# Where the intermediate word of a weight conversion lives: SBUF or PSUM

## The chip, the cores and the metric

One core of one Trainium2 chip runs the kernel. The metric is device time in microseconds (us), the median of three runs. The engines are called by the profile's names: PE (TensorE's matmuls), PEld (its weight loads), DVE (VectorE), ACT (ScalarE), POOL (GpSimd) and SP (SyncE, which issues most transfers).

## What is computed

Three layers follow each other. Attention has 4 sequences of 576 positions and 8 heads of 64, and each position sees the 64 positions up to its own. Its output, 2304 tokens of 512, goes through a dense layer, and that through a layer in which each token may choose one of eight experts:

```python
scores = scale * np.matmul(q, k.transpose(0, 1, 3, 2))
scores = np.where((rel >= 0) & (rel < 64), scores, -1000000000.0)
attn = np.exp(scores - max) / sum;  x = attn @ v          # (2304, 512)
h = x @ w_in                                              # 512 -> 2048, float64 weights
x = (np.maximum(h, 0.0) ** 2) @ w_out                     # 2048 -> 512
# experts: tokens with x @ w_skip > 0 take the expert of their largest gate logit
out = x.copy()
out[do_compute] = xc + gate_w * (np.maximum(xc @ w1[e], 0) @ w2[e])
```

The dense layer's weights come in as 64-bit numbers. Their two 32-bit words must be turned into a 32-bit float on the chip, before they can be multiplied.

## The kernel before

The 2304 tokens are 18 tiles of 128 and 9 chunks of two tiles. Attention of a tile is done in two groups of four heads' blocks. `at_qk` (L244) makes the scores in one PSUM bank, takes the row maximum on DVE (L268), the exponentials on ACT (L281), and normalizes on DVE (L285 to L288); `at_tr` (L292) transposes them into a bank that ACT reads out (L298); `at_pv` (L301) multiplies by v and splits the result into a high and a low part (ACT L322, DVE L323).

The dense layer runs in units (chunk, j) with eight j per chunk. `l1` (L447) takes 24 matmuls into a hidden bank (L443 to L445, tile `h`), ACT applies relu (L456) and square (L462), rounds to the high part (L463), and DVE makes the low part `gl` (L464). `l2` (L467) adds the products with the output weights to the accumulators `acc`. Units of chunks 0 and 1 alternate; l2 follows l1 by two units.

The conversion works on half a weight block at a time, 128 x 512 numbers: 32 halves in all, in the order i0, i1, o0, i2, o1, i3 and so on (i for input weights, o for output weights). `conv_load` (L184) orders a load of 512 KB on SP; five are under way at the start, and each conversion orders the next one when its last instruction is issued (L221, with a small GpSimd memset L193 behind it). `conv_next` (L199) turns a half into two float parts:

1. ACT L207 scales the high word, POOL L208 clamps it. Both work in place on `hw`.
2. DVE L210 shifts the high word left by 3 into `f`; DVE L212 merges the sign bit from `hw` into `f`; DVE L214 merges the top bits of the low word `lw` into `f`.
3. ACT L220 rounds `f` to the high part of the weight, POOL L221 subtracts to get the low part.

`f` is a tile of 128 x 512 words in SBUF, from a pool of NST = 3 buffers. Four conversions are called in the prologue (`PRO`: after steps 2, 4, 6 and 8 of ten, in which the eight groups of chunks 0 and 1 pass through `at_qk`, `at_tr` and `at_pv`). After that `inject` (L613) calls two in each unit: 4 in the first two units, and 24 in the next twelve.

PSUM has eight banks. Two belong to `ps_h` (hidden tiles, and the scores of chunks 0 and 1), two each to `ps_acc` and `ps_s` (accumulators of chunks 0 and 1, and their `at_pv`), and two to the pool `ps_a`. `psa()` (L91) hands out the tiles of `ps_a`, named `a`: the transpositions of all chunks and, from chunk 2 on, the scores and products of attention, and later the routing. The two banks of `ps_a2` are added only after the conversions. In `inject`, the attention of chunk 2 begins in the eleventh unit: its scores stand in units 10 to 13, ahead of those units' conversions, with the transposition of group n just ahead of the scores of group n + 1.

The last part of the kernel (L733 and L910) is in an order written by hand. All that comes before, the conversions among it, is put in order by a planner that goes by the order of the program as priority and by its own costs of instructions. On each engine the order is then fixed, and semaphores are the only waits.

Of the kernel before, what the change touches and what calls it, by code (L numbers as in the profile page):

```python
# [11 lines left out]
I32 = mybir.dt.int32  # L12
U32 = mybir.dt.uint32
AF = mybir.ActivationFunctionType
ALU = mybir.AluOpType
# [42 lines left out]
SIGN = -(1 << 31)  # L58
# [3 lines left out]
def body(ctx, tc, qt_d, kt_d, vw_d, wi_d, wo_d, w9_d, w9r_d, w1_d, w2_d, out):  # L62
# [28 lines left out]
    def psa():  # L91
        turn[0] += 1
        return ps_a[turn[0] // 2 % len(ps_a)].tile([P, 512], F32, tag="a", name="a")
# [90 lines left out]
    def conv_load(after=None):  # L184
        if not conv_q:
            return
        kind, j, half = conv_q.pop(0)
        tag = f"s{conv_n[0]}"
        conv_n[0] += 1
        raw = wp.tile([P, 512, 2], I32, tag=tag, name=f"r{kind}{j}_{half}")  # L190
        if after is not None:
            with tc.issue_after(after.ins):
                nc.gpsimd.memset(raw[:, 0, :], 0)  # L193
        nc.sync.dma_start(
            out=raw.rearrange("p a b -> p (a b)"),
            in_=(wi_d if kind == "i" else wo_d)[j, :, half * 1024:(half + 1) * 1024])
        raw_q.append((raw, tag, kind, j, half))

    def conv_next():  # L199
        if not raw_q:  # L200
            return
        raw, tag, kind, j, half = raw_q.pop(0)
        hw, lw = raw[:, :, 1], raw[:, :, 0]
        f = st.tile([P, 512], I32, tag="f", name="f")
        ff = f.bitcast(F32)
        hf = hw.bitcast(F32)
        nc.scalar.activation(out=hf, in_=hf, func=AF.Copy, scale=F64_SCALE)  # L207
        nc.gpsimd.tensor_scalar(  # L208
            out=hf, in0=hf, scalar1=F64_MAX, scalar2=-F64_MAX, op0=ALU.min, op1=ALU.max)
        nc.vector.tensor_scalar(  # L210
            out=f, in0=hw, scalar1=3, scalar2=None, op0=ALU.logical_shift_left)
        nc.vector.scalar_tensor_tensor(  # L212
            out=f, in0=hw, scalar=SIGN, in1=f, op0=ALU.bitwise_and, op1=ALU.bitwise_or)
        nc.vector.scalar_tensor_tensor(  # L214
            out=f, in0=lw, scalar=29, in1=f,
            op0=ALU.logical_shift_right, op1=ALU.bitwise_or)
        w_tag[kind, j, half] = tag
        w = wp.tile([P, 2, 512], F32R, tag=tag, name=f"w{kind}{j}_{half}")
        (wi_t if kind == "i" else wo_t)[j, half] = w
        nc.scalar.copy(out=w[:, 0, :], in_=ff)  # L220
        conv_load(nc.gpsimd.tensor_tensor(  # L221
            out=w[:, 1, :], in0=ff, in1=w[:, 0, :].bitcast(F32), op=ALU.subtract))
# [349 lines left out]
    if True:  # L572
# [27 lines left out]
        for s in range(10):  # L600
            if s < 8:
                qk[s]()
            if 1 <= s < 9:
                tr[s - 1]()
            if 2 <= s:
                pv[s - 2]()
            for _ in range(PRO[s]):
                conv_next()
# [4 lines left out]
        def inject(u, s):  # L613
            for op in slots.pop((u, s), ()):
                op()
            for _ in range(2 if u < 2 else 1):
                conv_next()
            v = u - first[NCH - 1]
            if v >= 0 and s == 1:
                for _ in range(EWV[v] if v < len(EWV) else 0):  # L620
                    ew_split()
                ew_pump(3 if v < NJ else NE + 1)

        n_u = len(units)
        for u in range(n_u):
            if u == first[2]:
# [5 lines left out]
                    out=w9b, in_=w9r_d.unsqueeze(0).to_broadcast([P, NE + 1, DM]))  # L632
# [100 lines left out]
        with tc.manual_schedule():  # L733
# [9 lines left out]
            for j in range(NJ - TAIL + 1, NJ - 1):  # L743
# [30 lines left out]
                out=id0, in0=pick, scalar1=float(FAR), scalar2=nearf, op0=ALU.add, op1=ALU.min)  # L774
# [4 lines left out]
                out=cnt, in0=pc[:, 0:NE], scalar1=float(P - 1), scalar2=None, op0=ALU.add)  # L779
            nc.vector.tensor_scalar(  # L780
                out=cnt, in0=cnt, scalar1=7, scalar2=None, op0=ALU.logical_shift_right)
# [187 lines left out]
```

## Time and profile before

| what | value |
|---|---|
| median of 3 runs | 689.13 us (687.75 to 691.53) |
| profiled execution | 687.76 us, its span 686.1 us |
| PE busy | 652.7 us, 95% of the span |
| DVE busy | 435.3 us, 63% |
| ACT busy | 355.1 us, 52% |
| POOL busy | 157.2 us, 23% |

The profile is one execution. Busy time is the time in which an engine works on an instruction; an instruction that stands still on a shared resource counts as busy. The shares are means over stages that have different limits, so the stretches and their waits are what is to be read.

### The profile page before, as it was taken

What the parts mean: (1) busy time and instruction counts of PE and PEld (TensorE: products, weight loads), DVE (VectorE), ACT (ScalarE), POOL (GpSimd) and SP (SyncE); (2) the same over time, 40 slices, a digit from 0 to 9 for tenths busy, and PEclk for the clock granted to TensorE, in tenths of its full rate; (3) what the DMA queues carried; (4) which work ended last, traced back from release to release, by engine and by line L of the source; (5) the groups of instructions that cost most, each with busy time, mean ns of one, the idle gap of its engine ahead of it and who ended that gap; (6) DMA issues with size and microseconds to landing.
All of it is one profiled execution on the core that took longest, in us unless ns stands there. A gap on an engine that the chain in (4) does not pass through costs nothing. (4 is left out here: it accounts for less than half of the span.)

```text
span 686.1 us, 12318 instructions
## 1 busy us (share of the span) xinstructions
PE 652.7 (95%) x4473; PEld 567.2 (83%) x4473; DVE 435.3 (63%) x1192; ACT 355.1 (52%) x819; POOL 157.2 (23%) x183
## 2 busy tenths in 40 slices
PE   6688999899999999999999999999999999999995
PEld 4577888789899999989899889989997777777774
DVE  5999999947726725824933942961644635278991
ACT  4776557544535535444444544453542535367861
POOL 5546566500100000000000010030011423024451
PEclk9899999999999999999999999999999999999999
DMA  8975344163213113122220310306584237738800
GB/s 293 266 234 192 124 154 141 45 230 102 55 46 101 48 54 89 44 70 68 64 70 31 101 41 30 114 19 208 192 280 166 63 125 277 297 116 294 305 15 8
DMA packets 51076, 88.70 MB, mean 129 GB/s; under 512 B 24046, under 2 KB 24302, under 8 KB 50864
## 3 DMA queue, kind: packets, MB, share of 16 engines
q1 hardware_dynamic: 47584, 83.38, 36.6%
q0 software_dynamic: 2976, 3.95, 1.8%
q8 instruction: 46, 0.75, 0.5%
q10 hardware_dynamic: 432, 0.32, 0.1%
q14 instruction: 38, 0.31, 0.1%
HBM read 79.07 MB, written 12.49 MB: 133 GB/s over the span
## 5 line engine op out<-in xcount | busy, mean ns | idle before, releaser
L443 PE MATMUL h<-xt,wi 128*128 128x256 f32 x576 | 164.1, 285 | 2.4 <-ACT r L456 2.4
L444 PE MATMUL h<-xt,wi 128*128 128x256 f32 x576 | 164.5, 286 | 0.0
L445 PE MATMUL h<-xt,wi 128*128 128x256 f32 x576 | 163.5, 284 | 0.0
L443 PE MATMUL acc<-wo,gh 128*128 128x512 f32 x288 | 115.9, 406 | 5.6 <-ACT wo L220 4.6
L443 PEld LDWEIGHTS h<-xt,wi 128*128 128x128 f32 x576 | 110.0, 191 | 6.0 <-ACT r L456 3.0
L444 PE MATMUL acc<-wo,gh 128*128 128x512 f32 x288 | 113.2, 394 | 0.1
L445 PE MATMUL acc<-wo,gl 128*128 128x512 f32 x288 | 112.6, 392 | 0.0
L444 PEld LDWEIGHTS h<-xt,wi 128*128 128x128 f32 x576 | 110.0, 191 | 2.5
L464 DVE TENSOR_TENSOR gl<-r,gh 128x512 fp32r<-128x512 f32 x72 | 53.8, 747 | 90.4 <-ACT gh L463 90.4
L445 PEld LDWEIGHTS h<-xt,wi 128*128 128x128 f32 x576 | 110.0, 191 | 0.5 <-POOL wi L221 0.2
L435 POOL DMA_INDIRECT tab_d<-route,posi x18 | 19.5, 1083 | 355.6 <-DVE posi L426 263.7
L456 ACT ACTIVATE r<-h 128x512 f32<-128x512 f32 x72 | 42.5, 594 | 97.8 <-PE h L445 94.1
L354 DVE CUSTOM_DVE_ANT_0 prod<-sm,w9b 128x512 f32<-128x512 f32 x108 | 73.9, 684 | 1.9 <-ACT sm L331 1.5
L443 PEld LDWEIGHTS acc<-wo,gh 128*128 128x128 f32 x288 | 53.9, 189 | 15.3 <-ACT wo L220 5.3
L445 PEld LDWEIGHTS acc<-wo,gl 128*128 128x128 f32 x288 | 54.1, 188 | 12.1 <-DVE gl L464 0.4
L444 PEld LDWEIGHTS acc<-wo,gh 128*128 128x128 f32 x288 | 54.4, 189 | 8.5 <-POOL wo L221 0.2
L521 DVE TENSOR_TENSOR e_s<-e_s,e_s 128x1024 fp32r<-128x1024 f32 x34 | 45.6, 1361 | 12.2 <-ACT e_s L519 11.8
L281 ACT ACTIVATE sm<-sm,nmx 128x128 f32<-128x128 f32 x96 | 37.5, 392 | 20.7 <-DVE nmx L275 20.3
L462 ACT ACTIVATE r<-r 128x512 f32<-128x512 f32 x72 | 45.3, 632 | 1.4
L298 ACT COPY sm<-a 128x512 f32<-128x512 f32 x36 | 21.2, 588 | 46.9 <-PE a L296 46.9
L463 ACT CAST gh<-r 128x512 fp32r<-128x512 f32 x72 | 44.5, 619 | 1.5
L519 ACT CAST e_s<-e_s 128x1024 fp32r<-128x1024 f32 x42 | 43.0, 1051 | 2.5 <-PE acc L445 2.0
(200 smaller groups left out, 1154.0 us busy)
## 6 DMA issues: line engine op xcount, KB each, us to landing
e_s<-in_w_dram SPq DMA_DIRECT2D x54, 512.0 KB, 5.5
v<-in_vw_dram SPq DMA_DIRECT2D x18, 512.0 KB, 3.6
ri<-in_wi_dram SPq DMA_DIRECT2D x16, 512.0 KB, 5.3
ro<-in_wo_dram SPq DMA_DIRECT2D x16, 512.0 KB, 3.5
k<-in_kt_dram SPq DMA_DIRECT2D x18, 384.0 KB, 3.9
e_r<-in_w_dram SPq DMA_DIRECT2D x10, 512.0 KB, 6.4
qpad<-in_qt_dram SPq DMA_DIRECT2D x36, 128.0 KB, 3.6
x_d<-sm SPq DMA_DIRECT2D x17, 256.0 KB, 2.1
```

Of the source, the lines that this page charges most:

```text
L281: nc.scalar.activation(out=e[:, u, :], in_=s[:, u * P:(u + 1) * P] if early else e[:, u, :], func=AF.Exp, bias=nmx[:, u:u + 1], scale=1.0 ...
L298: nc.scalar.copy(out=pt, in_=pp)
L354: nc.vector.tensor_tensor_reduce(out=prod, in0=x2_t[t], in1=w9b_t[0][:, j, :], scale=1.0, scalar=0.0, op0=ALU.mult, op1=ALU.add, accum_out ...
L443: nc.tensor.matmul(out_ap, lhsT=ah, rhs=bh, start=start, stop=False)
L444: nc.tensor.matmul(out_ap, lhsT=ah, rhs=bl, start=False, stop=False)
L445: nc.tensor.matmul(out_ap, lhsT=al, rhs=bh, start=False, stop=stop)
L456: nc.scalar.activation(out=r, in_=hp.rearrange("p a b -> p (a b)"), func=AF.Relu)
L462: nc.scalar.activation(out=r, in_=r, func=AF.Square)
L463: nc.scalar.copy(out=ghf, in_=r)
L464: nc.vector.tensor_tensor(out=glf, in0=r, in1=ghf.bitcast(F32), op=ALU.subtract)
L519: nc.scalar.copy(out=hi, in_=raw)
L521: eng.tensor_tensor(out=lo, in0=raw, in1=hi.bitcast(F32), op=ALU.subtract)
```

## The change

The intermediate word gets a tile `fp` from `psa()`, read as 32-bit integers. L210 writes `fp` instead of `f`; L212 reads and writes `fp`; L214 reads `fp` and writes `f` in SBUF as before. The other inputs (`hw`, `lw`) stay in SBUF, and ACT L220 and POOL L221 read `f` as before. 32 tiles more are drawn from the two banks of `ps_a`.

```diff
         hw, lw = raw[:, :, 1], raw[:, :, 0]
+        fp = psa().bitcast(I32)
         f = st.tile([P, 512], I32, tag="f", name="f")
...
         nc.vector.tensor_scalar(
-            out=f, in0=hw, scalar1=3, scalar2=None, op0=ALU.logical_shift_left)
+            out=fp, in0=hw, scalar1=3, scalar2=None, op0=ALU.logical_shift_left)
         nc.vector.scalar_tensor_tensor(
-            out=f, in0=hw, scalar=SIGN, in1=f, op0=ALU.bitwise_and, op1=ALU.bitwise_or)
+            out=fp, in0=hw, scalar=SIGN, in1=fp, op0=ALU.bitwise_and, op1=ALU.bitwise_or)
         nc.vector.scalar_tensor_tensor(
-            out=f, in0=lw, scalar=29, in1=f,
+            out=f, in0=lw, scalar=29, in1=fp,
             op0=ALU.logical_shift_right, op1=ALU.bitwise_or)
```

## Rows read from the trace of the kernel before

**Rows 1.** Stretches: from:to, length, busy PE, PEld, DVE, ACT, POOL (count), PEclk, DMA, GB/s.
```profile
10.00:36.00 26.00, 17.86 (x148) 14.98 (x149) 23.61 (x44) 20.07 (x81) 12.40 (x17) 0.80 1.00 312
36.00:142.00 106.00, 97.79 (x717) 86.50 (x714) 99.04 (x126) 68.63 (x159) 61.39 (x74) 1.00 0.44 143
...
200.00:500.00 300.00, 300.00 (x2231) 271.60 (x2230) 166.23 (x690) 144.65 (x374) 15.78 (x22) 1.00 0.25 79
```

**Rows 2.** Waits of PE, 36 to 142 us: total us, times, longest us.
```profile
PE acc L443 <- ACT wo L220: 4.6, 4, 1.4
PE h L443 <- ACT r L456: 2.4, 1, 2.4
PE a L296 <- DVE sm L288: 1.1, 2, 0.7
```

**Rows 3.** Waits of PE, 8 to 36 us.
```profile
PE a L296 <- DVE sm L288: 3.2, 4, 1.3
```

**Rows 4.** Waits of ACT, 8 to 142 us.
```profile
ACT wo L220 <- DVE f L214: 13.1, 9, 3.1
```

**Rows 5.** DVE groups by form, 0 to 142 us: count, busy us, mean ns, idle before.
```profile
L214 DVE SCALAR_TENSOR_TENSOR f<-ri,f 128x512 int32<-128x512 int32 x16 | 17.9, 1120 | 0.3
L214 DVE SCALAR_TENSOR_TENSOR f<-ro,f 128x512 int32<-128x512 int32 x16 | 17.1, 1070 | 0.4
L212 DVE SCALAR_TENSOR_TENSOR f<-ri,f 128x512 int32<-128x512 int32 x16 | 16.1, 1004 | 0.4
L212 DVE SCALAR_TENSOR_TENSOR f<-ro,f 128x512 int32<-128x512 int32 x16 | 14.6, 915 | 0.3
L464 DVE TENSOR_TENSOR gl<-r,gh 128x512 fp32r<-128x512 f32 x15 | 14.5, 967 | 3.7 <-ACT gh L463 3.7
...
L210 DVE TENSOR_SCALAR f<-ro 128x512 int32<-128x512 int32 x16 | 11.8, 739 | 0.6 <-POOL ro L208 0.6
L210 DVE TENSOR_SCALAR f<-ri 128x512 int32<-128x512 int32 x16 | 8.3, 517 | 0.3 <-POOL ri L208 0.3
```

**Rows 6.** DVE groups by form, 142 to 500 us.
```profile
L464 DVE TENSOR_TENSOR gl<-r,gh 128x512 fp32r<-128x512 f32 x54 | 37.2, 689 | 80.2 <-ACT gh L463 80.2
```

**Rows 7.** Timeline of DVE, 60 to 65 us: start, duration, instruction.
```profile
60.50 1.65 DVE L214 SCALAR_TENSOR_TENSOR f<-ri,f 128x512 int32<-128x512 int32 x1
62.07 0.41 DVE L210 TENSOR_SCALAR f<-ro 128x512 int32<-128x512 int32 x1
```

**Rows 8.** Timeline of POOL, 60 to 65 us.
```profile
60.19 1.41 POOL L221 TENSOR_TENSOR wi<-f,wi 128x512 fp32r<-128x512 f32 x1 [1.32 <-ACT wi L220]
```

**Rows 9.** Lines 323 (0 to 142 us), 268, 331: ns min/median/max, first/last start.
```profile
L323 DVE TENSOR_TENSOR xt<-xp,xt x8: 386/408/411, 19.0 to 55.3; 128x256 fp32r<-128x256 f32 x8
...
L268 DVE TENSOR_REDUCE nmx<-s x8: 676/680/692, 8.1 to 35.4; 128x4 f32<-128x512 f32 x8
...
L331 DVE COPY sm<-acc x9: 680/687/692, 144.0 to 520.8; 128x512 f32<-128x512 f32 x9
```

**Rows 10.** Stretches, tile f alone: busy DVE, ACT, POOL; the clock and DMA are whole.
```profile
10.00:36.00 26.00, 11.71 (x16) 3.23 (x5) 7.02 (x5) 0.80 1.00 312
36.00:142.00 106.00, 73.21 (x80) 16.82 (x27) 37.86 (x27) 1.00 0.44 143
```

**Rows 11.** Timeline of PE: a transposition and the next group's scores, chunk 2.
```profile
58.43 0.60 PE L296 MATMUL a<-ident,sm 128*128 128x128 f32 x4
58.86 0.38 PE L249 MATMUL a<-maskb,identb 128*128 128x512 bf16 x1
```

**Rows 12.** Timeline of PE: first matmuls of the second unit, and of l2.
```profile
41.44 0.36 PE L443 MATMUL h<-xt,wi 128*128 128x256 f32 x1
...
46.94 0.48 PE L443 MATMUL acc<-wo,gh 128*128 128x512 f32 x1
```

**Rows 13.** Timeline of ACT: the last two transpositions of chunks 0 and 1 read out.
```profile
43.33 0.59 ACT L298 COPY sm<-a 128x512 f32<-128x512 f32 x1
...
47.40 0.58 ACT L298 COPY sm<-a 128x512 f32<-128x512 f32 x1
```

## The prediction

> **What bounds the kernel now.** I first read the busy times by stretch [rows 1]. From 200 to 500 us TensorE is busy 300.0 of 300 us; there it alone sets the pace, and whatever is gained ahead of it arrives at the end undiminished. The stretch with the weight conversion is another matter: from 36 to 142 us VectorE is busy 99.0 of 106 us and TensorE 97.8, so both are near full and 8.2 us of TensorE are idle. From 10 to 36 us, the attention of the first two chunks, TensorE is busy 17.9 of 26 us and the DMA share is 1.00.
>
> Next, what ended TensorE's waits. From 36 to 142 us [rows 2] it is the high half of an output weight (ACT L220) for 4.6 us, the relu that empties a hidden bank (ACT L456) for 2.4 us, and the softmax product (DVE L288) for 1.1 us: 8.1 of the 8.2 us. The first two go back to VectorE: ScalarE's copy L220 sat 13.1 us waiting for DVE L214 [rows 4], and the relu is queued behind such a copy. So here VectorE, by way of ScalarE, sets the end. From 8 to 36 us [rows 3] DVE L288 alone ends 3.2 us of waits.
>
> Why is VectorE full? The form rows [rows 5] show three conversion instructions of the same 128x512 size with means of 1.0 to 1.1 us (L214), 0.9 to 1.0 us (L212) and 0.5 to 0.7 us (L210), and L464 at 967 ns. The same L464 takes 689 ns after 142 us [rows 6], when GpSimd is almost idle. One case close up: L214 starts at 60.50 us and takes 1.65 us [rows 7], while GpSimd's L221 runs from 60.19 for 1.41 us [rows 8]; L214 ends 0.55 us after L221. It stood still while GpSimd read. Instructions of VectorE with one input or the only tensor input in PSUM, in the same stretch, do not show this [rows 9]: L323 (PSUM and SBUF) at most 411 ns in 8, L268 (PSUM) at most 692 ns in 8.
>
> **The change part by part.**
>
> *L212 and L214.* Their second input moves to PSUM, which makes them the kind of L323. Before: 17.9 + 17.1 + 16.1 + 14.6 = 65.7 us for 64 [rows 5]. After: 64 x 0.687, the PSUM copy L331 of the same size [rows 9], = 44.0. Gain of VectorE time 21.7 us. Bounds: 0 if they go on waiting, because hw and lw still come from SBUF; 21.7 if none waits. I take 21.7, the end that L323 is nearest to.
>
> *L210.* It writes PSUM. Before: 11.8 + 8.3 = 20.1 us for 32 [rows 5]; undisturbed it takes 0.41 us [rows 7], a rate that no PSUM instruction of this size shows. After: 32 x 0.687 = 22.0, a loss of 1.9 us. Bounds: 32 x 0.41 = 13.1, a gain of 7.0, if it keeps its rate and never waits; 20.1 + 32 x 0.277 = 29.0, a loss of 8.9, if it loses its rate and still waits. I take 22.0: every VectorE row with PSUM runs at 0.68 or more.
>
> Sum: 19.8 us of VectorE time, between a loss of 8.9 and a gain of 28.7. No row has VectorE writing PSUM; that is the weakest price here.
>
> [...]
>
> *Where it lands.* Of the 96 instructions 80 lie between 36 and 142 us with 73.2 us [rows 10]; at 0.687 each they are 55.0, so VectorE falls from 99.0 to 80.8 of 106 us, below TensorE's 97.8. TensorE is late next, and the gain is capped by its waits of [rows 2]: 8.1 us, not 18. Between 10 and 36 us the 16 others go from 11.7 [rows 10] to 11.0: I count nothing there. The cover for everything else is TensorE's own work, 97.8 us; if it ran out, the next 18 us of VectorE would count in full.
>
> *The bank.* Each of the 32 conversions now draws one of attention's two PSUM banks, in the order of the program. That the order is kept can be seen on TensorE: the second group of chunk 2 (L249) starts 0.43 us after the transposition that stands before it in the program [rows 11], though the other bank had been read out by 47.98 us [rows 13], and the two further pairs (81 and 117 us) look alike. So L210 waits for whoever reads the tile two turns back (ACT L298 or the four exponentials L281), and behind L210 on VectorE stand L464, L288, L268 and L323, for which ScalarE and TensorE wait. In turn a transposition waits on TensorE's queue for L214, with the layer matmuls behind it. Bounds: nothing, and the 7.2 us of the first rival. I take one such reader, 0.59 us [rows 13], for each of the four groups of chunk 2: 2.4 us. No DMA is moved by itself, but each conversion still issues the next weight load from SP after L221, so loads move with the conversions: later where they wait for a bank, earlier where they are faster. The instructions outside the hand-ordered tail are ordered by a planner with its own costs, so the order may shift too; rows of before cannot price that, and it widens the range only.
>
> Net: 8.1 - 2.4 = 5.7 us. The profiled execution took 687.76 us, 1.7 of them outside the span; it becomes 682.1. It lies 1.4 below the median of the runs, 689.13, so the forecast in the median's terms is 683.4.
>
> **The rivals.**
>
> *Weights late because of the banks (slower).* In program order the conversions of the prologue stand between the transpositions: the fourth follows the seventh's bank, the fifth the eighth's. Those banks are read out at 43.33 + 0.59 = 43.9 and 47.40 + 0.58 = 48.0 us [rows 13]. With three instructions of 0.687, a copy of about 0.6 and L221 at 1.4 us [rows 8] the second half of weight 1 is ready at 48.0 where TensorE wants it at 41.44, and both halves of output weight 0 (two conversions) at 54.1 where it wants them at 46.94 [rows 12]: 7.2 us late. If half of the 7.0 us of later waits [rows 2] then comes back, the kernel is 3.7 us slower: 692.8. It decides if attention keeps its pace. Against it: four conversions held back leave VectorE 4 x 3 x 0.687 = 8.2 us more for attention before 45 us, and the DMA share of 1.00 [rows 1] eases, since held conversions order no further weights; from about 4 us of earlier transpositions on, the rival is gone.
>
> *The waits change their name (no change).* Chunk 2's attention, which today starts well ahead of its place in the program and fills idle TensorE [rows 11], must now queue behind 24 conversions (4 of the prologue, 4 of the first two units, 16 of the next eight) for its first bank. For it: between two of its groups stand two conversions on two banks, so L210 meets a bank that four exponentials read. If bank waits eat what L220 gives back, all but 0.6 us: 688.5.
>
> *All of it arrives.* The bank costs nothing and the prologue's 3.2 us [rows 3] return as well: 689.1 - 11.3 = 677.8.
>
> *The change does not do what it says.* L212 and L214 go on waiting for GpSimd and only L210's 8.9 us are added to a nearly full VectorE: 698 at most, 695 if some is hidden. L323, never held in 8, speaks against it.
>
> **How the numbers follow.** Forecast (680 to 686.5) 0.45; all of it (below 680) 0.14; the waits change their name (686.5 to 690.5) 0.20; late weights (690.5 to 697) 0.16; does not do it 0.05. A measurement of this kernel can tell about 0.5% from no change, so faster means below 685.7 and slower above 692.6. Faster: 0.14 and most of 0.45, 0.55. Slower: two thirds of 0.16 and the 0.05, with a little for a new order, 0.18. The rest, 0.27, is within. The range takes in the upper gain and the slower rival's middle: 677.5 to 693.5.
>
> **What would show it.** Right: L212 and L214 near 0.69 us without ones of 1.6; L210 also near 0.69; VectorE below 85 us between 36 and the end of conversion; the waits of TensorE for L220 and L456 mostly gone; everything after the conversions some 6 us earlier. Wrong: L210 idle for ACT L298 or L281 by more than 3 us in total; the second weight's matmuls after 44 us; conversions still at 1 us and more; or a TensorE that idles just as long for another reason.

## The result: 0.74% slower, with a cheaper conversion

The changed kernel takes 694.25 us (12 runs, 691.97 to 695.92) where the kernel before takes 688.85 (12 runs): ratio 1.0074, interval 1.0057 to 1.0091. The forecast was 683.4 us, faster; the time lies outside its range of 677.5 to 693.5. The profiled execution has a span of 692.0 us where that of before has 686.1.

The lines below are numbered as in the changed kernel: one more than before from L204 on (L211, L213, L215 are the three VectorE instructions, L221 and L222 the two parts of the weight, L465 the low part gl, L299 the copy of a transposition).

First the stretches, with the columns of [rows 1]:

```profile
10.00:36.00 26.00, 19.57 (x178) 16.86 (x178) 18.23 (x42) 21.32 (x90) 7.61 (x11) 0.87 0.98 300
36.00:142.00 106.00, 94.73 (x626) 84.08 (x625) 74.44 (x116) 63.34 (x135) 54.53 (x78) 0.95 0.44 142
...
200.00:500.00 300.00, 300.00 (x2243) 271.51 (x2242) 162.43 (x671) 143.97 (x371) 15.28 (x22) 1.00 0.25 78
```

VectorE is relieved, even more than forecast (80.8): 74.4 of 106 us instead of 99.0, in part because 116 of its instructions fall into the stretch instead of 126. TensorE, which should have filled up, is busy 94.7 us instead of 97.8, does 626 matmuls instead of 717 in the same 106 us, and was granted a clock of 0.95 instead of 1.00. From 200 to 500 us it is busy without a gap in both kernels. VectorE's last copy of the dense layer's accumulators tells how late the kernel is after that (L332, which is L331 in [rows 9]; first and last start stand behind the durations):

```profile
L332 DVE COPY sm<-acc x9: 681/686/693, 152.7 to 525.6; 128x512 f32<-128x512 f32 x9
```

It starts at 525.6 us instead of 520.8. So 4.8 us of the span's 5.9 are lost ahead of it and, as TensorE is full from 200 to 500 us, most likely ahead of 200 us. The other 1.1 us come in the last stage of these two executions, where the clock granted from 564.8 to 604.8 us was 0.96 and in the same work before (560 to 600 us) 1.00; whether the change has a part in that, no run shows.

The groups of VectorE from 0 to 150 us, as in [rows 5]:

```profile
L465 DVE TENSOR_TENSOR gl<-r,gh 128x512 fp32r<-128x512 f32 x16 | 14.6, 916 | 17.0 <-ACT gh L464 17.0
L213 DVE SCALAR_TENSOR_TENSOR a<-ro,a 128x512 int32<-128x512 int32 x16 | 11.1, 693 | 0.3
L213 DVE SCALAR_TENSOR_TENSOR a<-ri,a 128x512 int32<-128x512 int32 x16 | 11.1, 691 | 0.3
L211 DVE TENSOR_SCALAR a<-ri 128x512 int32<-128x512 int32 x16 | 11.0, 688 | 2.4 <-POOL ri L209 1.0 <-POOL ro L209 0.8 <-ACT sm L299 0.6
L211 DVE TENSOR_SCALAR a<-ro 128x512 int32<-128x512 int32 x16 | 11.0, 688 | 9.7 <-issue 4.8 <-POOL ro L209 4.7
L215 DVE SCALAR_TENSOR_TENSOR f<-ro,a 128x512 int32<-128x512 int32 x16 | 10.9, 684 | 0.5
L215 DVE SCALAR_TENSOR_TENSOR f<-ri,a 128x512 int32<-128x512 int32 x16 | 10.9, 681 | 0.5
```

The six groups sum to 66.0 us, to the tenth what the prediction had. None is stretched by GpSimd any more (the longest of the 96 takes 697 ns), and writing PSUM alone (L211, 688 ns on average) costs here what reading it alone costs (L215, 681 and 684). But the idle time on the right has grown: VectorE now waits 17.0 us for ScalarE's L464 ahead of gl, and 9.7 us ahead of L211. Of these, 4.7 us are waits for a half that GpSimd has not yet clamped (L209); what "issue" hides is shown further down.

What TensorE waits for, 36 to 160 us, as in [rows 2]:

```profile
PE h L444 <- ACT wi L221: 6.5, 5, 1.9
PE acc L444 <- ACT gh L464: 1.9, 1, 1.9
PE h L445 <- DVE xt L324: 1.6, 1, 1.6
PE acc L444 <- ACT wo L221: 0.6, 1, 0.6
```

Output weights (4.6 us before) hardly hold it now; input weights do, for 6.5 us, which held it nowhere in [rows 2]. The conversions became cheaper and the weights later.

How late, is told by GpSimd's L222, the last instruction of a conversion. The fourth and the fifth conversion in the kernel before (there L221):

```profile
29.29 1.34 POOL L221 TENSOR_TENSOR wi<-f,wi 128x512 fp32r<-128x512 f32 x1 [3.48 <-ACT wi L220]
...
32.63 1.28 POOL L221 TENSOR_TENSOR wo<-f,wo 128x512 fp32r<-128x512 f32 x1 [0.94 <-ACT wo L220]
```

and in the changed one:

```profile
45.19 1.28 POOL L222 TENSOR_TENSOR wi<-f,wi 128x512 fp32r<-128x512 f32 x1
...
46.47 1.28 POOL L222 TENSOR_TENSOR wo<-f,wo 128x512 fp32r<-128x512 f32 x1
```

15.9 and 13.8 us later. Ahead of the first gl, VectorE had finished 8 conversions before (at 46.0 us) and has finished 3 now (at 40.8 us; at 46.0 us it has finished 5). This lead, weights converted ahead of their use, is what the kernel has lost. That is the first rival of the prediction. What remained to be shown is that the turn of the bank does it and nothing else about the change, why the lead is not won back by conversions that are now faster, and what the blocked attention of chunk 2 costs.

### The profile page after: what moved, and what is told of

Its sections match the earlier page's. It is cut to its first block, busy times and chain, and to the rows that moved or that the text cites. A ratio compares the mean times of both kernels' runs of the same rounds, so it can differ in the third digit from the quotient of the medians.

```text
span 692.0 us, 12325 instructions
## 1 busy us (share of the span) xinstructions
PE 657.3 (95%) x4473; PEld 570.8 (82%) x4473; DVE 412.6 (60%) x1192; ACT 355.1 (51%) x819; POOL 149.4 (22%) x183
## 5 line engine op out<-in xcount | busy, mean ns | idle before, releaser
L444 PE MATMUL h<-xt,wi 128*128 128x256 f32 x576 | 166.1, 289 | 6.9 <-ACT wi L221 6.5
L445 PE MATMUL h<-xt,wi 128*128 128x256 f32 x576 | 166.2, 289 | 1.6 <-DVE xt L324 1.6
L446 PE MATMUL h<-xt,wi 128*128 128x256 f32 x576 | 165.0, 287 | 0.0
L444 PEld LDWEIGHTS h<-xt,wi 128*128 128x128 f32 x576 | 111.6, 194 | 12.1 <-ACT wi L221 8.6
L465 DVE TENSOR_TENSOR gl<-r,gh 128x512 fp32r<-128x512 f32 x72 | 53.2, 740 | 103.6 <-ACT gh L464 103.6
L445 PEld LDWEIGHTS h<-xt,wi 128*128 128x128 f32 x576 | 111.8, 194 | 3.6 <-DVE xt L324 1.8
L446 PEld LDWEIGHTS h<-xt,wi 128*128 128x128 f32 x576 | 111.7, 194 | 0.5
L457 ACT ACTIVATE r<-h 128x512 f32<-128x512 f32 x72 | 42.2, 596 | 110.5 <-PE h L446 97.3
L299 ACT COPY sm<-a 128x512 f32<-128x512 f32 x36 | 21.2, 588 | 52.1 <-PE a L297 52.1
L463 ACT ACTIVATE r<-r 128x512 f32<-128x512 f32 x72 | 44.8, 632 | 1.2
L464 ACT CAST gh<-r 128x512 fp32r<-128x512 f32 x72 | 44.2, 621 | 1.3
```

The lines of the kernel that those rows point to most:

```text
L299: nc.scalar.copy(out=pt, in_=pp)
L444: nc.tensor.matmul(out_ap, lhsT=ah, rhs=bh, start=start, stop=False)
L445: nc.tensor.matmul(out_ap, lhsT=ah, rhs=bl, start=False, stop=False)
L446: nc.tensor.matmul(out_ap, lhsT=al, rhs=bh, start=False, stop=stop)
L457: nc.scalar.activation(out=r, in_=hp.rearrange("p a b -> p (a b)"), func=AF.Relu)
L463: nc.scalar.activation(out=r, in_=r, func=AF.Square)
```

## The experiments

Each time is a median; each ratio is to the kernel before, run on the same chip between the others, with its 95% interval. Where a diff is against the changed kernel, `psa` is its drawing from the two shared banks.

### Is it the place in the rotation, or the word in PSUM?

The two banks are parted: attention has one, the conversions the other, until the last conversion; then both serve attention again.

```diff
-    ps_a = [pool("ps_a", 2, space=PSUM)]
+    ps_a = [pool("ps_a", 1, space=PSUM)]
+    ps_f = pool("ps_f", 1, space=PSUM)
...
-        return ps_a[turn[0] // 2 % len(ps_a)].tile(...)
+        return ps_a[turn[0] % len(ps_a)].tile(...)
...
-        fp = psa().bitcast(I32)
+        fp = ps_f.tile([P, 512], F32, tag="a", name="fp").bitcast(I32)
...
+                ps_a.append(ps_f)      # at first[2], after the last conversion
...
-                ps_a.append(pool("ps_a2", 2, space=PSUM))
+                ps_a.extend([pool("ps_a2", 2, space=PSUM)] * 2)
```

> The word stays in PSUM, but in a bank of its own: the two banks of attention are divided, one for attention, one for the conversions until they are done. If the place in attention's rotation is what costs (conversions wait behind transpositions, the attention of chunk 2 waits behind conversions), the shorter VectorE instructions now show: 680 to 686 us, the three instructions at 0.69 us, eight conversions ahead of the first gl as in the kernel before, and the attention of chunk 2 starting near 46 us. If the word in PSUM is itself what costs (a planner's order made for longer instructions, VectorE standing behind ScalarE), it stays at 692 or more.

Measured: 681.45 us, ratio 0.9893 (0.9872 to 0.9914). The stretch from 36 to 142 us (columns as above), and all that TensorE waited for in it:

```profile
36.00:142.00 106.00, 103.25 (x717) 92.37 (x716) 76.06 (x123) 68.89 (x156) 53.01 (x74) 0.98 0.43 142
...
PE a L298 <- ACT sm L300: 1.9, 1, 1.9
PE a L316 <- ACT sm L300: 0.7, 1, 0.7
```

No wait for a weight is left, TensorE idles 2.75 of 106 us, and VectorE has finished nine conversions ahead of the first gl. The same three instructions, the same words in PSUM: the rival that the word itself costs has fallen. The gain that the prediction forecast is there, and the rotation turned it into a loss.

The control has the parted banks and the word in SBUF (the diff above without the line of `fp`, on the kernel before).

> The control of the run with a bank of its own: the word in SBUF as in the kernel before, but attention has one bank until the conversions are done; the other lies idle. It prices one bank less for attention. Both theories: 688 to 692 us (0 to 3 more than the kernel before); if it is over 693, the run with a bank of its own carries that price too and must be read against this one.

Measured: 691.93 us, 1.0045 (1.0028 to 1.0063). One bank less for attention costs some 3 us, so the gain of the word in PSUM in a bank of its own, against this control, is about 10.5 us: 1.0045 less 0.9893, 1.5%.

### Which conversions make the loss?

The change was split: the four conversions of the prologue, and the 28 later ones.

```diff
-        fp = psa().bitcast(I32)
+        fp = psa().bitcast(I32) if len(conv_c) >= 4 else None    # other run: < 4
+        conv_c.append(1)
...
+        fp = f if fp is None else fp
```

> The change for 28 conversions; the four of the prologue keep their word in SBUF and take no turn in the banks. If the loss is made in the prologue (conversions behind transpositions, their lead lost for good), this is at or below the kernel before: 684 to 689 us. If it is made where the attention of chunk 2 must wait behind conversions, it stays at 692 to 695.

Measured: 684.83 us, 0.9938 (0.9916 to 0.9959).

> The other half: only the four conversions of the prologue have their word in PSUM in the rotation, 28 have it in SBUF. If the prologue makes the loss, 692 to 696 us (the lead is lost and the later conversions are slow as well). If the attention of chunk 2 makes it, 688 to 690 us, since that is free to start early again.

Measured: 694.46 us, 1.0073 (1.0048 to 1.0098). The four conversions of the prologue alone make the whole loss; without them the change is a gain. Attention of chunk 2 starts early in this run, at 41.4 us, so its delay is not what makes this loss:

```profile
41.36 0.39 PE L253 MATMUL a<-maskb,identb 128*128 128x512 bf16 x1
```

The effects do not add: 28 words in PSUM give 4.1 us when the prologue is in order and nothing (694.25 against 694.46) when it is not.

### Is it the turn alone?

In the kernel before, the four conversions of the prologue keep their word in SBUF and only take their turn of a bank, by one column written and read ahead of L210 and one written behind L214. The copy into `f` makes L210 follow.

```diff
+        fp = psa().bitcast(I32) if len(conv_c) < 4 else None
+        conv_c.append(1)
+        if fp is not None:
+            nc.vector.memset(fp[:, 0:1], 0)
+            nc.vector.tensor_copy(out=f[:, 0:1], in_=fp[:, 0:1])
...
+        if fp is not None:
+            nc.vector.tensor_copy(out=fp[:, 1:2], in_=f[:, 0:1])
         w_tag[kind, j, half] = tag
```

> The word stays in SBUF everywhere, with the three instructions as in the kernel before, but each of the four conversions of the prologue takes a turn of attention's banks all the same: one column is written before its first instruction and one after its last (three instructions of one column each, under 0.5 us together, twelve in all). If the turn alone delays the conversions and makes the loss, 692 to 697 us, as with the four words in PSUM (694.46). If it takes the word in PSUM itself, 688 to 690 us.

Measured: 695.4 us, 1.0081 (1.0061 to 1.0101). The fourth conversion's turn on VectorE's timeline:

```profile
38.47 0.06 DVE L209 MEMSET a<- 128x1 int32 x1 [0.34 <-ACT sm L306]
38.63 0.16 DVE L210 COPY f<-a 128x1 int32<-128x1 int32 x1
```

It begins at 38.47 us, released by L306, the copy of a transposition (L298 in the kernel before); in the kernel before, the same conversion began at 24.1 us. With the three instructions working in SBUF alone, and one column of the bank touched, the loss is the same. It is the turn: the conversion starts when that copy ends, at once. What the planner's new order of all the rest adds, the runs do not take apart.

### Why the lead is not won back

Once past the prologue, three instructions of 0.69 us could run ahead of TensorE's matmuls. VectorE's timeline in the changed kernel shows two things that stop them:

```profile
38.76 0.69 DVE L211 TENSOR_SCALAR a<-ri 128x512 int32<-128x512 int32 x1 [0.65 <-ACT sm L299]
...
54.16 0.70 DVE L211 TENSOR_SCALAR a<-ro 128x512 int32<-128x512 int32 x1 [4.67 <-POOL ro L209]
...
75.33 0.69 DVE L211 TENSOR_SCALAR a<-ri 128x512 int32<-128x512 int32 x1
80.02 1.37 DVE L465 TENSOR_TENSOR gl<-r,gh 128x512 fp32r<-128x512 f32 x1 [4.00 <-ACT gh L464]
81.31 0.68 DVE L213 SCALAR_TENSOR_TENSOR a<-ri,a 128x512 int32<-128x512 int32 x1
```

At 54.16 us VectorE had been idle for 4.67 us: the next half was not yet clamped, because its load is ordered only by an earlier conversion. And at 75 us a conversion's first instruction is done while its second (81.31) stands in the queue behind a gl that comes 4.0 us later: gl waits for ScalarE, ScalarE for TensorE's matmuls, and TensorE for an input weight. Nobody in this ring is ahead, so each round waits for the one before.

The link at ScalarE is worth a close look, because VectorE is not late there. The word of the input weight in question was ready at 75.41 us (L215), and ScalarE stood idle from 73.99 to 76.30 us. But the weight's high part L221 stands in its queue behind the relus L457 and the squares L463 of two units, and it starts only at 78.85 us. From VectorE, ScalarE (two lines) and TensorE:

```profile
74.72 0.69 DVE L215 SCALAR_TENSOR_TENSOR f<-ri,a 128x512 int32<-128x512 int32 x1
76.30 1.09 ACT L457 ACTIVATE r<-h 128x512 f32<-128x512 f32 x2 [2.31 <-PE h L446]
78.85 0.61 ACT L221 CAST wi<-f 128x512 fp32r<-128x512 f32 x1
79.52 0.39 PE L444 MATMUL h<-xt,wi 128*128 128x256 f32 x1 [1.93 <-ACT wi L221]
```

The waits that end at 94.44 us (1.93 us) and 107.89 us (0.82 us) look alike: the words were ready at 89.43 and 104.36 us, and L221 started at 93.79 and 107.23 us. So 4.7 of the 6.5 us of waits for input weights are also owed to ScalarE's fixed order, and not to a word that VectorE had late. No run here changes that order by itself.

The late loads were tried in two ways. With eight loads at the start instead of five (`LOOK = 8`):

> The changed kernel with eight weight loads ordered at the start instead of five, all else equal. After the late prologue VectorE stands idle at 49.5 us for 4.7 us until GpSimd's clamp of the ninth half, whose load is only ordered by a late conversion. If the lead is not won back because loads are late, this gives 689 to 692 us. If it is not won back because the order on VectorE ties conversions to the low parts gl, it stays at 693 to 696 us; three more loads in the busy first 36 us can also delay k and v, which would make it slower than the changed kernel.

Measured: 687.76 us, 0.9979 (0.9967 to 0.9991), 0.95% below the changed kernel. Now VectorE has finished 9 conversions ahead of the second gl (at 61.7 us) and 17 ahead of the sixth (at 84.2 us); in the changed kernel it was 8 (at 56.6 us) and 15 (at 80.0 us). TensorE waits 2.5 us for input weights instead of 6.5:

```profile
PE h L444 <- ACT wi L221: 2.5, 2, 1.4
PE h L445 <- DVE xt L324: 1.6, 1, 1.6
```

The control, eight loads in the kernel before:

> Control for the changed kernel with eight loads (687.76, 6.5 below the changed kernel): the kernel before with eight loads. If the loads matter because the changed kernel has lost its lead, the kernel before gains nothing: 688 to 693 us. If more loads are simply better, it gains as much: 682 to 685 us.

Measured: 687.33 us, 0.9961 (0.9949 to 0.9974). This was not expected: more loads help the kernel before as well, by 0.39%. So of the 0.95% about 0.56%, some 3.9 us, is owed to the lost lead. Put the other way: with eight loads in both kernels, the change costs 0.18% (0.9979 less 0.9961) instead of 0.74%, and the intervals overlap.

The other way leaves the first 36 us alone: the fifth to the seventh conversion order two loads each.

```diff
-        conv_load(nc.gpsimd.tensor_tensor(
-            out=w[:, 1, :], in0=ff, in1=w[:, 0, :].bitcast(F32), op=ALU.subtract))
+        ins = nc.gpsimd.tensor_tensor(
+            out=w[:, 1, :], in0=ff, in1=w[:, 0, :].bitcast(F32), op=ALU.subtract)
+        conv_c.append(1)
+        for _ in range(2 if 5 <= len(conv_c) <= 7 else 1):
+            conv_load(ins)
```

> The changed kernel; the fifth, sixth and seventh conversion order two loads each instead of one, so that from about 55 us on eight are under way, and the first 36 us keep their five. If late loads after the prologue keep the lead from being won back, 685 to 689 us, the prologue's own delay of some 5 us staying in part; if the gain with eight loads at the start came from their early place or from another order, 692 to 695 us.

Measured: 690.67 us, 1.0005 (0.9985 to 1.0026), with a wide spread of runs (687.02 to 695.6). That lies between the two expectations. Against 1.0074 the gain of 0.7% is clear, and it comes with the first five loads unchanged: late loads probably keep a part of the lead from being won back. How much of it these loads would give the kernel before was not run.

Both were also put on the kernel with a bank of its own:

> The bank of its own (681.45 us) and eight loads at the start. If conversions there are still held up by loads, 677 to 680 us; if their lead is kept already (nine conversions ahead of the first gl, 2.6 us of TensorE waits left from 36 to 142 us), the three loads only crowd the first 36 us: 681 to 686 us.

Measured: 686.16 us, 0.9954 (0.9927 to 0.9981): slower than without them (0.9893). The first layer matmul starts at 38.1 us instead of 34.9, which fits the crowding of the first 36 us that was expected (the DMA share there is 0.92 with five loads), but is not shown to come from it.

> The same two loads for three conversions, with the bank of its own. No crowding of the first 36 us. If loads still hold conversions up there: 678 to 681 us; if not, 681 to 683 us, the same as without them (681.45).

Measured: 680.42 us, 0.9852 (0.9812 to 0.9893), not distinguishable from 0.9893 by the intervals. That loads no longer hold anything up where the lead is kept fits this, but is not shown: the middle of the interval is 0.4% lower.

### How far the turn reaches, and what chunk 2 costs

These runs try other arrangements. In the first, attention has both banks in the prologue (four words in SBUF); then 28 conversions have one for themselves.

```diff
+    ps_f = pool("ps_f", 1, space=PSUM)
+    ps_a.append(ps_f)                  # psa() alternates: turn[0] % len(ps_a)
...
+        fp = ps_f.tile([P, 512], F32, tag="a", name="fp").bitcast(I32) if len(conv_c) >= 4 else None
...
+        ps_a.pop()                     # after the prologue; appended again at first[2]
```

> In the prologue attention has both banks and the four conversions keep their word in SBUF; after it the 28 conversions have one of the two banks for themselves until they are done, attention the other. Against the run with a bank of its own throughout (681.45) this gives the prologue its second bank back and leaves four words in SBUF. If one bank is felt in the prologue: 679 to 681 us. If the one bank is felt only by the attention of chunk 2: 681 to 683 us.

Measured: 684.05 us, 0.9922 (0.9895 to 0.9949). It is above both expectations; that it is slower than a bank of its own throughout (0.9893) is not certain, as the intervals overlap. The fifth conversion on VectorE's timeline, and its end on GpSimd's:

```profile
43.87 0.69 DVE L216 TENSOR_SCALAR fp<-ro 128x512 int32<-128x512 int32 x1 [1.45 <-ACT sm L304]
...
47.85 1.30 POOL L227 TENSOR_TENSOR wo<-f,wo 128x512 fp32r<-128x512 f32 x1 [7.88 <-ACT wo L226]
```

Its bank had served a transposition of the prologue, and it waited for L304, the copy of that. The turn reaches one conversion past the four.

In the next run, conversions 24 to 31 go back to SBUF, and attention alternates over both banks throughout.

> As the last, but conversions 24 to 31, from the unit on in which the attention of chunk 2 stands, have their word in SBUF again, and attention alternates over both banks there: scores in the free one, transpositions in the other, behind conversion 23. If the attention of chunk 2 in one bank is the price that the control with one bank paid (2.96 us over the kernel before), this takes some of it back: 678 to 681 us. If the eight conversions that wait for GpSimd again cost more, 682 to 685 us.

Measured: 688.22 us, 0.9984 (0.9964 to 1.0003): worse than both expectations. It has the same late fifth conversion, its last eight conversions have their word in SBUF again, where in the kernel before L214 and L212 took 0.9 to 1.1 us [rows 5], and chunk 2's transpositions begin only at 113 us (52 in the run before), since they must follow conversion 23 in its bank.

So the first eight words were kept in SBUF, once with the bank of its own after that, once with the rotation.

> As the run with a bank of its own after the prologue (684.05), but the first eight conversions keep their word in SBUF, so that no conversion of the first two units follows a transposition of the prologue in a bank. If that turn of the fifth conversion made the 2.6 us over the bank of its own throughout (681.45): 680 to 682 us, with the fifth half ready near 34 us. If it was something else: 683 to 685 us.

Measured: 679.51 us, 0.9874 (0.9858 to 0.9891), the lowest median of all (by its ratio the run with late loads, 0.9852, is lower, within its interval). Against 0.9922 the gain is clear. The fifth conversion ends in time again:

```profile
32.75 1.28 POOL L227 TENSOR_TENSOR wo<-f,wo 128x512 fp32r<-128x512 f32 x1 [0.95 <-ACT wo L226]
```

and from 36 to 142 us TensorE is nearly full (columns as above, then its waits):

```profile
36.00:142.00 106.00, 104.41 (x771) 93.19 (x771) 81.04 (x128) 70.90 (x160) 55.33 (x74) 1.00 0.47 153
...
PE a L302 <- DVE sm L294: 1.1, 2, 0.7
PE h L449 <- ACT xt L328: 0.5, 1, 0.5
```

> As the run with the prologue's four words in SBUF and 28 in the rotation (684.83), but with the first eight in SBUF. If the turn of the fifth conversion behind the last transposition costs there as well: 681 to 683.5 us. If what is left is the attention of chunk 2 that waits behind conversions (its first group at 100 us instead of 46): 684 to 686 us.

Measured: 685.46 us, 0.9957 (0.9941 to 0.9972), not below 0.9938 with four words in SBUF. Here the turn of the fifth conversion is not what is left. The first scores of chunk 2 on TensorE's timeline:

```profile
96.53 0.39 PE L253 MATMUL a<-maskb,identb 128*128 128x512 bf16 x1
```

They start at 96.53 us where they start at 46.27 with the bank of its own. Only the banks after the eighth conversion differ in the program of these two runs, so attention of chunk 2 and conversions in turn on the same banks cost 0.83% (0.9957 less 0.9874), some 6 us. Probably that is because attention comes late, when TensorE could have done it in its gaps; what conversions lose by waiting for attention is in the same 6 us.

## Why the prediction was wrong, step by step

**The view of the bound** was right. VectorE held up the weights, with L214 and L212 at 0.9 to 1.1 us beside GpSimd [rows 5] where they took 0.68 to 0.69 in the changed kernel; with that gone and the lead kept, TensorE idles 1.6 us from 36 to 142 us and the kernel takes 679.5 us. The cap of 8.1 us from [rows 2] was close: that run gains 1.26% of 688.7, 8.7 us.

**The prices of L212, L214 and L210** were right: 66.0 us foreseen, 66.0 measured, from rows of an instruction that only reads PSUM (L331, 687 ns [rows 9]). The last digit is luck, as the groups lie from 681 to 693 ns around the 687 that was used. Those with one of two tensor inputs in PSUM took 681 to 693 ns, against 689 for L464 with both in SBUF [rows 6].

**The term of the bank** is the step that failed. It was set at 2.4 us, four reads of 0.59 us in chunk 2, and the place where the loss is made, the prologue, was left to a rival with a chance of 0.16. What the runs show in place of the 2.4 us is 1.8% between the rotation and a bank of its own (1.0074 less 0.9893), some 12.5 us. That rival had the mechanism, the size (692.8 against 694.25) and the times nearly right: the second half of weight 1 was foreseen at 48.0 us and is ready at 46.5 (45.19 + 1.28).

In chunk 2 itself the waits for a reader were under-sized, too. Two of VectorE's idle times ahead of L211, 3.49 and 1.32 us, carry no releaser in the profile ("issue"), but both end 0.1 us after a copy of a transposition, L299. The first, with the copy ahead of it:

```profile
130.78 0.59 ACT L299 COPY sm<-a 128x512 f32<-128x512 f32 x1 [2.53 <-PE a L297]
131.45 0.70 DVE L211 TENSOR_SCALAR a<-ro 128x512 int32<-128x512 int32 x1 [3.49 <-issue]
```

Read as waits for the bank, they are 4.8 us, and with 0.6 us in the prologue 5.4: the sign of being wrong that was set at 3 us for L210.

**What was held against that rival** is the reasoning to look at. It said that the rival is gone once the transpositions come some 4 us earlier. They did come earlier: the last two start at 37.4 and 38.1 us instead of 41.1 and 45.0 [rows 13 show their copies before], probably because VectorE had fewer conversions in front. The conversions were late all the same, because they had not only the bank to wait for. ScalarE's queue shows the next link:

```profile
43.81 0.68 ACT L208 ACTIVATE ri<-ri 128x512 f32<-128x512 f32 x1 [2.98 <-DMA ri<-in_wi_dram]
44.38 0.60 ACT L221 CAST wi<-f 128x512 fp32r<-128x512 f32 x1
```

The fourth conversion's word had been ready since 42.07 us (L215, 41.39 + 0.68), but its high part L221 stands behind L208 of a later half, which waited 2.98 us for a load that a late conversion had ordered late. The prediction said that the loads move with the conversions, and did not price it: what holds conversions back also holds back the loads of later ones, and a late load blocks an in-order queue for a conversion that is ready.

**The rival that the waits change their name** is partly seen, too: attention of chunk 2 starts at 105.8 us instead of 46.1, as its condition had it:

```profile
105.78 0.39 PE L250 MATMUL a<-maskb,identb 128*128 128x512 bf16 x1
```

It was to eat the gain but for 0.6 us of the 8.1. With the first eight conversions in order, attention and conversions in turn cost some 6 us, so its size was nearly right. It was priced as an alternative to the first rival, and here both came at once.

**The chances.** Two mechanisms of the same kind, conversions behind attention and attention behind conversions, had been foreseen, and each was given its chance (0.16 and 0.20) as if the other were absent. "Slower" had 0.18. Each new tile in a rotation of two is a wait in both directions; that deserved more than the gain's leftover.

**What stays open.** Of the 5.9 us of span, TensorE's busy time is 4.6 (657.3 against 652.7) and its idle time 1.3. Part of the busy time is a lower granted clock, described below. But the run with only the prologue's four words in PSUM loses as much (0.73%) without a lower mean clock: four executions at 0.986 to 0.994 (mean 0.989), where eight of the kernel before beside them had 0.982 to 0.991 (mean 0.988). So the clock is not what the loss hangs on, though in that run too it was 0.97 from 36 to 142 us. Part is the planner's new order, which changes with each of these edits. The splits above are differences between whole kernels, each with an order of its own.

## What to carry to other kernels

When a temporary is moved into a shared rotation of buffers, its instructions can be priced from rows, as they were here; what decided here is the order of turns, and which queue or load stands behind each turn. List, for every new tile, who reads the tile before it in that buffer and when, first of all in the prologue, where a lead is built that later stages live on. If the temporary needs one buffer, try one of its own, even at the cost of one less for its neighbour: here that turned +0.74% into -1.07%, and from the ninth conversion on into -1.26%.

## What the runs showed of the hardware

Three VectorE instructions of 128x512 words that read or write PSUM take 681 to 693 ns each on average, whether PSUM is the output, the second input or both, and none of the 96 was held by GpSimd (longest 697 ns); with all operands in SBUF two of them took 0.9 to 1.1 us in the same company [rows 5]. The shift lost its faster rate: 0.41 us undisturbed from SBUF to SBUF [rows 7], 0.688 with its output in PSUM.

TensorE's granted clock fell in the changed kernel where it had not before. Its timeline after a wait of 1.56 us:

```profile
42.46 0.58 PE L445 MATMUL h<-xt,wi 128*128 128x256 f32 x1 [1.56 <-DVE xt L324]
42.84 0.41 PE L446 MATMUL h<-xt,wi 128*128 128x256 f32 x1
43.05 0.41 PE L444 MATMUL h<-xt,wi 128*128 128x256 f32 x1
```

Until about 49 us matmuls start 0.21 us apart instead of 0.12, and the clock from 36 to 60 us is 0.86 of full speed, from 60 to 100 us 0.96; before, it was 1.00 in both. The 24 matmuls that the profile shows in this time, at 0.21 instead of 0.12, are 2.2 us more, an estimate of what this stretch cost at most, since TensorE had to wait for weights afterwards as well. The sum of idle time does not by itself tell whether the clock falls: the kernel before idled 8.2 us from 36 to 142 us [rows 1] at a clock of 1.00, the one with a bank of its own 2.75 us at 0.98. Nor does the length of one wait by itself: the kernel before waited longer, and its clock from 60 to 100 us was 1.00 all the same:

```profile
63.41 0.39 PE L443 MATMUL h<-xt,wi 128*128 128x256 f32 x1 [2.35 <-ACT r L456]
```
